# Eleven instead of eight attention chunks get q and k rearranged in DRAM and turned in 32x32 blocks on VectorE

## The chip, the cores and the metric

The kernel runs on one core of one Trainium2 chip. The metric is device time in microseconds for one execution of the whole program, as the median of several runs. The times of before are 1193.07 to 1195.81 us over nine runs, median 1193.97 us.

## What is computed

A block-wise linear attention with decay (batch 4, 8 heads, 768 tokens, head dimension 64) feeds a mixture of four two-layer experts over its 3072 output rows of 512 values. All data is fp32.

```python
# attention, per block of the sequence; the result is the same for any block length
intra = ((q_b @ k_b.T) * Dmask) @ v_b           # Dmask[i, j] = lam**(i-j) for i >= j
inter = (q_b * lam_pow) @ kv_state
out_b = intra + inter
kv_state = lam_block * kv_state + (k_b * rev_pow).T @ v_b
# bridge: (B, H, S, D) -> x of (B*S, H*D)
# experts: p = normalised domain_probs
for e in range(4):
    out += p[:, e:e+1] * (maximum(x @ w1[e], 0) @ w2[e])   # 512 -> 1024 -> 512
```

## The kernel before

**Tiling.** The 3072 tokens are 24 chunks `n` of 128 (`C`); a batch has 6 chunks (`NCH`), so chunk `n` is batch `b` and place `c` with `b, c = divmod(n, 6)`. Eight chunks make a group `g` (`CPG = 8`), three groups in all. A group's attention output, transposed, is the tile `xT` of 1024 columns, and the experts run on a group at a time as units `(g, e)`. Both expert products use Strassen's scheme with seven products (`M1` to `M7`); each first product is nested once more, so it reads seven 128x256 operand pieces of x and seven of w1. Those pieces are made once (on GpSimd or VectorE), stored to DRAM as `x_ops` and `w_ops`, and loaded again for each product.

**Order of the work.** The schedule is written out by hand. A loop goes over units, in each over seven products `i`, in each over eight slots `x`. A slot puts a few matmuls of the second product of this unit (L860) and of the first product of the next unit (L806) on TensorE, and then serves queues:

- `feed` (L733, L735) issues the loads `xs_in` and `ws_in` for the first product after next, once per product. Both tiles have two buffers, so a load waits until TensorE has read the tile of two products ago.
- `feed2` (L841) issues the two `w2t` loads of a later second product.
- `background`, through `rest()`, is one deferred piece of VectorE work per slot (the sums `hS` that the second product reads, masks, state updates). `soon` puts pieces at its head.
- `steps` is the attention of the next group: for each chunk `turn`, then `scores`, then `values`. `values` of chunk `n` is followed by `load_more(n + 2)`.
- `chores` and `pump` hand out GpSimd's preparation of weights and the stores of it.
- `results` issues the stores of finished output rows (L878).
- `trickle` issues one waiting `across` piece at every odd slot.

Nearly all DMAs are issued from SyncE (SP), in program order.

**The two ways of turning q and k.** The scores need q and k with the head dimension on partitions. In the ordinary way `load` (L123) brings q and k of a chunk with tokens on partitions; `turn` puts eight 128x128 transposes on TensorE (L530), into two PSUM banks, and ScalarE copies both to SBUF (L535, L536).

In the other way, taken by chunks with `comes_across(n)`, `bring_across(b)` lists 32 DRAM-to-DRAM copies for batch `b` (q then k; four quarters; four head pairs), which put 32x32 blocks of q and k where the later load wants them. Each copy (L367) covers all chunks from `ACROSS[b]` to the batch's end, in elements of 32 values (128 bytes). `load_across` (L384) brings `qx` and `kx` of a chunk, `turn_across` puts two `nc.vector.transpose` of 128x512 (L517) on VectorE, which turn the 32x32 blocks in place, and there is neither a TensorE transpose nor a ScalarE copy. Token-major `kn` and `vn` are loaded in both ways.

`bring_across(2)` is called before the last direct products of group 0, `bring_across(3)` at unit 3. If pieces still wait when a chunk of this kind is loaded, `load_more` issues all of them first:

```python
def load_more(n):
    if not comes_across(n):
        load(n)
    else:
        trickle(len(pieces))
        load_across(n)
        load(n, "kv")
```

DMAs issued from SP use eight semaphores in turn, so each waits for the landing of the eighth before it; a load of what another DMA has written to DRAM also waits for that landing.

Of the kernel before, what the change touches and what calls it, by code (L numbers as in the profile page):

```python
# [22 lines left out]
def kernel(  # L23
# [329 lines left out]

    ACROSS = {2: 2, 3: 2}
    across = dram.tile([B, 2, P, NHP, NCH * 4, 32], FP32, name="across")
    pieces = []

    def bring_across(b):  # L360
        c = ACROSS[b]
        for x, of in enumerate((q, k)):
            for y in range(4):
                for ac in range(NHP):
                    src = of[b, 4 * (y // 2) + ac, c * C:, (y % 2) * 32:(y % 2 + 1) * 32]
                    to = across[b, x, y * 32:(y + 1) * 32, ac, c * 4:]
                    pieces.append(lambda to=to, src=src: nc.sync.dma_start(  # L367
                        out=to, in_=src.rearrange("(t p) d -> p t d", p=32),
                    ))
# [6 lines left out]
    def comes_across(n):  # L376
        b, c = divmod(n, NCH)
        return b in ACROSS and c >= ACROSS[b]

# [986 lines left out]
```

## Time and profile before

| what | value |
|---|---|
| median of nine runs | 1193.97 us |
| the profiled execution's own time | 1193.68 us |
| its span | 1191.9 us |
| TensorE (PE) busy | 1179.3 us, 99% |
| weight loads (PEld) | 1023.3 us, 86% |
| VectorE (DVE) busy | 807.2 us, 68% |
| ScalarE (ACT) busy | 253.2 us, 21% |
| GpSimd (POOL) busy | 636.6 us, 53% |
| DMA queue of SP | 252144 packets, 320.40 MB, 81.1% of 16 engines |
| packets under 512 B | 117280 of 261783 |
| TensorE transposes of q and k (L530) | 128 in 16 chunks |
| VectorE block turns (L517) | 16 in 8 chunks |
| copies to `across` (L367) | 64 of 64 KB |

The span is what the profile covers, from the first instruction to the last; the run's own time lies 1.8 us above it. Matmuls are pipelined: the duration of one is longer than the distance from its start to the next one's start, and only the latter is time on TensorE.

### The profile page before, as it was taken

Reading aid. Unit: us, or ns where it says so; the run is one execution under the profiler, and the core shown is the slowest. Engines: PE = TensorE matmul, PEld = TensorE weight load, DVE = VectorE, ACT = ScalarE, POOL = GpSimd, SP = SyncE. Lnnn points to the kernel's source line nnn. Section 1 sums busy time; section 2 is a strip of 40 time slices with the busy share of each in tenths; the row PEclk is TensorE's granted clock in tenths of the full one; section 3 lists DMA queues with packets and bytes.
Section 4 is the critical chain, followed back from the end, with each engine's and each line's share of the span. In section 5 each row is a group of like instructions: output and inputs, shape, how many; then the busy total and the mean of one; then the engine's idle time right before and its main releaser. Section 6 shows DMA issues by size and latency. Waiting matters only on the chain.

```text
span 1191.9 us, 17827 instructions
## 1 busy us (share of the span) xinstructions
PE 1179.3 (99%) x6559; PEld 1023.3 (86%) x6559; DVE 807.2 (68%) x1334; ACT 253.2 (21%) x462; POOL 636.6 (53%) x600
## 2 busy tenths in 40 slices
PE   9998999999999999999999999999999999999998
PEld 8887888888888888888888888888888888888877
DVE  6597786477467857647756764764665676777784
ACT  3321121113201201311220120120143241240232
POOL 1966248449457900055244655415683683883884
PEclk9999999999999999999999999999999999999999
DMA  9896789999999997899997989998986657566542
GB/s 231 215 304 200 247 265 314 366 326 333 367 352 330 323 284 228 253 305 293 311 307 250 290 289 316 280 322 280 316 288 248 238 204 277 189 256 223 212 167 81
DMA packets 261783, 324.23 MB, mean 272 GB/s; under 512 B 117280, under 2 KB 203200, under 8 KB 261696
## 3 DMA queue, kind: packets, MB, share of 16 engines
q1 hardware_dynamic: 252144, 320.40, 81.1%
q10 hardware_dynamic: 9552, 2.69, 1.1%
q8 instruction: 52, 0.85, 0.3%
q14 instruction: 35, 0.29, 0.1%
HBM read 237.69 MB, written 89.54 MB: 275 GB/s over the span
## 4 chain that ended last, share of the span: by engine, by line
PE 86%; DVE 7%; DMA 2%; POOL 2%; issue 2%; ACT 0%; SPq 0%; ACTq 0%; DVEq 0%; POOLq 0%
PE pg L806 35%; PE q L860 29%; PE pq L1032 12%; DVE m L95 3%; PE sp L552 2%; DVE hS L95 2%; PE op L580 2%; PE pM L1124 1%; PE op L575 1%; POOL ops L95 1%; DVE xt L95 1%; PE op L588 1%; PE qp L530 1%; DMA w_ops<-w2o 1%; DMA w2b<-in_moe_w_dram 1%
## 5 line engine op out<-in xcount | busy, mean ns | idle before, releaser
L806 PE MATMUL pg<-xs_in,ws_in 128*128 128x256 f32 x1960 | 469.9, 380 | 1.7 <-DVE m L95 1.5
L806 PEld LDWEIGHTS pg<-xs_in,ws_in 128*128 128x128 f32 x1960 | 371.1, 190 | 54.4 <-DVE m L95 3.8
L95 DVE TENSOR_TENSOR m<-pg,m 128x512 f32<-128x512 f32 x451 | 307.9, 687 | 102.4 <-PE pg L806 94.4
L860 PE MATMUL q<-w2t,hS 128*128 128x256 f32 x1024 | 243.4, 380 | 0.0
L860 PEld LDWEIGHTS q<-w2t,hS 128*128 128x128 f32 x1024 | 193.2, 190 | 27.0 <-issue 0.2
L876 DVE SCALAR_TENSOR_TENSOR acc<-q,gate,acc 128x256 f32<-128x256 f32 x192 | 92.5, 482 | 169.6 <-PE q L860 169.3
L860 PE MATMUL q<-w2t,m 128*128 128x256 f32 x768 | 182.8, 381 | 0.0
L860 PEld LDWEIGHTS q<-w2t,m 128*128 128x128 f32 x768 | 144.7, 190 | 20.8 <-DVE m L95 0.4
L818 ACT ACTIVATE m<-m 128x512 f32<-128x512 f32 x132 | 83.0, 630 | 337.4 <-DVE m L95 332.8
L95 POOL TENSOR_TENSOR m<-m,xT 128x512 f32<-128x512 f32 x64 | 81.6, 1292 | 73.6 <-ACT m L818 55.2
L95 DVE TENSOR_TENSOR sums<-pq,sums 128x256 f32<-128x256 f32 x154 | 64.5, 422 | 45.7 <-PE pq L1032 39.9
L814 ACT COPY m<-pg 128x512 f32<-128x512 f32 x88 | 51.5, 586 | 177.7 <-PE pg L806 172.7
L95 POOL TENSOR_TENSOR kn<-kn,s_decay 128x512 f32<-128x512 f32 x20 | 23.8, 1191 | 120.1 <-DMA across<-in_k_dram 80.4
L1032 PE MATMUL pq<-acc,w2t 128*128 128x256 f32 x352 | 86.7, 379 | 0.5 <-POOL m L95 0.5
L95 DVE TENSOR_TENSOR m<-m,m 128x512 f32<-128x512 f32 x96 | 83.7, 875 | 0.0
L95 POOL TENSOR_TENSOR ops<-w2b 128x256 f32<-128x256 f32 x24 | 17.8, 762 | 117.3 <-DMA w2b<-in_moe_w_dram 116.4
L1032 PEld LDWEIGHTS pq<-acc,w2t 128*128 128x128 f32 x352 | 66.8, 190 | 9.9 <-POOL m L95 0.9
L753 ACT ACTIVATE m<-m 128x512 f32<-128x512 f32 x48 | 30.3, 631 | 167.6 <-DVE m L95 167.4
L95 DVE TENSOR_TENSOR hS<-m,m 128x512 f32<-128x512 f32 x64 | 54.6, 858 | 4.9 <-ACT m L818 4.9
L95 POOL TENSOR_TENSOR acc<-hT,hT 128x512 f32<-128x512 f32 x32 | 40.3, 1272 | 29.7 <-PE pq L1032 29.0
L95 POOL TENSOR_TENSOR w2o<-w2b 128x512 f32<-128x512 f32 x32 | 41.6, 1322 | 25.7 <-DMA w2b<-in_moe_w_dram 10.6
L95 POOL TENSOR_TENSOR acc<-hT,acc 128x512 f32<-128x512 f32 x32 | 40.7, 1273 | 7.4 <-PE pq L1032 5.4
(136 smaller groups left out, 1311.9 us busy)
## 6 DMA issues: line engine op xcount, KB each, us to landing
xs_in<-x_ops SPq DMA_DIRECT2D x70, 896.0 KB, 6.3
ws_in<-w_ops SPq DMA_DIRECT2D x70, 896.0 KB, 8.7
w2t<-w_ops SPq DMA_DIRECT2D x66, 256.0 KB, 6.7
w2t<-w_sums SPq DMA_DIRECT2D x64, 256.0 KB, 4.1
w_ops<-ops SPq DMA_DIRECT2D x28, 512.0 KB, 6.0
w2t<-in_moe_w_dram SPq DMA_DIRECT2D x48, 256.0 KB, 3.6
x_ops<-ops SPq DMA_DIRECT2D x17, 512.0 KB, 8.4
w2b<-in_moe_w_dram SPq DMA_DIRECT2D x32, 256.0 KB, 6.0
```

The costliest lines, as they stand in the source:

```text
L95: eng.tensor_tensor(out=o, in0=a, in1=b, op=op)
L530: nc.tensor.transpose(out=x[:, ac * C:(ac + 1) * C], in_=y[:, 2 * ac:2 * ac + 2].rearrange("p r d -> p (r d)"), identity=ident[:],)
L552: nc.tensor.matmul(out=sp[r][:, ac * C:(ac + 1) * C], lhsT=hc(kT)[half[r], ac], rhs=hc(qT)[half[r], ac], start=True, stop=True,)
L575: nc.tensor.matmul(out=op[r][half[x], a * C:(a + 1) * C], lhsT=kv[half[r], 2 * a + x], rhs=hc(qs)[half[r], 2 * a + x], start=(a == 0), sto ...
L580: nc.tensor.matmul(out=op[r][half[x], a * C:(a + 1) * C], lhsT=vn[:, 4 * r + 2 * a + x], rhs=hc(st[r])[:, 2 * a + x], start=(first and a = ...
L753: nc.scalar.activation(out=o[:], in_=o[:], func=AF.Relu)
L806: nc.tensor.matmul(out=p[:, j * 256:(j + 1) * 256], lhsT=ws[i][:, j * P:(j + 1) * P], rhs=xs[i], start=(fresh and j == 0), stop=True, skip ...
L814: nc.scalar.copy(out=new[at][:], in_=p[:])
L818: nc.scalar.activation(out=new[at][:], in_=new[at][:], func=AF.Relu)
L860: nc.tensor.matmul(out=p[:, s * DH:(s + 1) * DH], lhsT=h[A_OF[m]][:, c * 256 + s * P:c * 256 + (s + 1) * P], rhs=fed2[g, e, m][uu][:, c], ...
L876: nc.vector.scalar_tensor_tensor(out=o, in0=x, scalar=w, in1=o, op0=ALU.mult, op1=ALU.add)
L1032: nc.tensor.matmul(out=p[:, 0:256], lhsT=fed3[e, m, x // 2][:, x % 2, c * P:(c + 1) * P], rhs=b[B_OF[i]][:, c * 256:(c + 1) * 256], start= ...
```

## The change

One line is changed. It sets from which chunk of its batch on q and k come across.

```diff
-    ACROSS = {2: 2, 3: 2}
+    ACROSS = {2: 0, 3: 1}
```

Before, chunks 14 to 17 (batch 2) and 20 to 23 (batch 3) come across; after, also 12, 13 and 19. There are 64 copies to `across` as before, but each of the 32 for batch 2 covers six chunks instead of four (768 elements instead of 512), and each for batch 3 covers five instead of four (640 instead of 512). Since chunk 19 is loaded one chunk earlier than chunk 20, the copies of batch 3 that wait at that moment are issued there, one after the other.

## The prediction

> **What bounds the kernel now.** I read the page's busy times first, then the busy times by stretch, then TensorE's groups by shape, and last the timelines of PE and SP around the three chunks. For the whole span and for the stretches in which the three chunks are turned:
>
> ```profile
> PE 1179.3 (99%) x6559; PEld 1023.3 (86%) x6559; DVE 807.2 (68%) x1334; ACT 253.2 (21%) x462; POOL 636.6 (53%) x600
> ```
>
> ```profile
> 200.00:300.00 100.00, 100.00 (x629) 86.41 (x628) 63.50 (x103) 19.36 (x36) 62.67 (x66) 1.00 0.99 334
> 300.00:400.00 100.00, 99.87 (x610) 86.16 (x609) 68.29 (x108) 16.64 (x30) 63.09 (x61) 1.00 0.99 348
> 400.00:500.00 100.00, 99.50 (x547) 86.11 (x546) 65.92 (x109) 17.72 (x31) 15.72 (x17) 1.00 0.85 264
> 500.00:600.00 100.00, 100.00 (x609) 86.44 (x608) 64.77 (x107) 17.54 (x32) 42.04 (x47) 1.00 0.96 303
> ```
>
> The columns are the stretch, then us (and instructions) of PE, PEld, DVE, ACT and POOL, the granted clock and the DMA share. PE is full and at full clock, so what leaves PE shortens the run and what makes PE wait lengthens it. DMA at 0.99 is the second thing to watch. DVE at 0.64 to 0.68 has room. PE's idle time in the stretch from 300 to 700 us is small: its waits there are two, 1.0 us in all, both for a DVE evacuation.
>
> **Term 1: TensorE loses 24 transposes.** Groups by shape, and PE's timeline at a chunk that is still turned on PE:
>
> ```profile
> L530 PE MATMUL qp<-ident,qn 128*128 128x128 f32 x64 | 10.2, 283 | 0.0
> L530 PE MATMUL kp<-ident,kn 128*128 128x128 f32 x64 | 9.7, 274 | 0.0
> ```
>
> ```profile
> 492.81 1.89 PE L806 MATMUL pg<-xs_in,ws_in 128*128 128x256 f32 x8
> 494.54 0.60 PE L530 MATMUL qp<-ident,qn 128*128 128x128 f32 x4
> 494.98 0.60 PE L530 MATMUL kp<-ident,kn 128*128 128x128 f32 x4
> 495.41 1.89 PE L860 MATMUL q<-w2t,hS 128*128 128x256 f32 x8
> ```
>
> One transpose lasts some 280 ns, but they overlap: from the first (494.54) to the matmul after the eighth (495.41) it is 0.87 us, 109 ns each. The eight products ahead take 1.73 us (492.81 to 494.54), as always, so nothing else is hidden there. Three chunks free 3 x 0.87 = 2.6 us. The scores (L552) are the same instructions in both ways, so nothing is added to PE. I take this term at its full value, because PE is full at 272, 307 and 524 us, where chunks 12, 13 and 19 are turned.
>
> The Trainium skill (TensorE: Matmul & The Clock Gate, Part 4: PE-mode transpose) gives about 275 ns for a 128x128 transpose in a kernel's context. The duration in the rows agrees with it, but the distance from start to start does not; by the page, as an estimate, 24 x 275 ns would be 6.6 us. The sum goes by the 109 ns.
>
> ScalarE loses six copies of 0.59 us (L535, L536), and GpSimd's decay of `kn` no longer waits for PE. ScalarE is 21% busy, so both are worth nothing.
>
> **Term 2: VectorE gets six block turns.**
>
> ```profile
> L517 DVE STREAM_TRANSPOSE qx<-qx x8: 700/701/702, 339.4 to 653.7; 128x512 f32<-128x512 f32 x8
> L517 DVE STREAM_TRANSPOSE kx<-kx x8: 669/690/701, 340.6 to 655.0; 128x512 f32<-128x512 f32 x8
> ```
>
> Six at 0.70 us are 4.2 us, 1.4 us a chunk, put at the head of the deferred DVE work, so the sums `hS`, which the second product reads, come two slots later. After 307 us DVE idles 0.17 to 2.97 us ahead of each evacuation, 10 us in 14, and after 524 us nearly as much: there the cover is complete. After 272 us (chunk 12) it is 84 to 87% busy and the cover is thin. What it costs where the cover fails is in the trace: eight chunks already go this way, and while they do PE waits 1.0 us for DVE. If all of that is theirs, a chunk costs 0.12 us and three cost 0.4 us. Bounds: 0 (the cover holds), and 3 x 1.4 = 4.2 us (nothing hides); the second needs a full DVE, which the stretches exclude, so I use 0 to 1 us and take 0.4.
>
> **Term 3: more small packets on the DMA engines.** The copies to `across` get 32 x 256 + 32 x 128 = 12,288 more elements of 128 bytes. The trace has 32,768 such packets, 12.9 ns each on one engine, so the addition is 12,288 x 12.9 / 16 = 9.9 us of all 16 engines. Loading `qx` and `kx` (512 packets of 512 B each at 27.7 ns, 0.89 us) instead of q (1024 of 256 B at 18 ns, 1.15 us) adds 0.6 us a chunk. Two thirds of the 9.9 us fall between 63 and 176 us (share 0.80 to 0.86), where PE's few waits are for DVE, whose inputs are long there. SP is busy without a break from 63 to 83 us; ten longer copies push a store that GpSimd waits for (landing at 79.5 us) by some 2 us, and GpSimd's operands for the next products are ready 15 us early. I put that at nothing. In the full stretch from 200 to 400 us only the two bigger loads are new. The weight piece `ws_in` is the later half of each pair; across that stretch it lands 3.2 to 8.5 us before its first matmul, 3.2 us at the pair behind chunk 12's load. 0.6 us fits. Zero again, with 0 to 1.7 us as the range (chunks 12 and 13 give nothing if DMA were the limit).
>
> The Trainium skill (DMA: Bandwidth & Descriptors, Rules for kernel authors) says to coalesce small transfers, since below 64 KB one pays mostly overhead; that speaks against this change. Here the copies grow from 64 to 96 and 80 KB, so their per-copy part is paid no more often; it is the packet count that grows.
>
> **Term 4: the burst ahead of chunk 19.** This is the part that decides. SP's timeline where chunk 19 is loaded:
>
> ```profile
> 479.14 1.22 SPq L123 DMA_DIRECT2D qn<-in_q_dram  x2
> 480.40 1.73 SPq L123 DMA_DIRECT2D kn<-in_k_dram  x2
> 482.17 0.51 SPq L118 DMA_DIRECT2D vn<-in_v_dram  x1
> ...
> 485.09 1.08 SPq L841 DMA_DIRECT2D w2t<-in_moe_w_dram  x2
> 486.26 0.42 SPq L733 DMA_DIRECT2D xs_in<-x_ops  x1
> 486.73 0.42 SPq L735 DMA_DIRECT2D ws_in<-w_ops  x1
> ```
>
> In the changed program's instruction order ten copies of 640 elements come at 479.14, then `qx`, then `kx`, which waits for the landing of the ten, then `kn`, `vn`, an output store, two `w2t`, and only then `xs_in` and `ws_in` of the product that starts at 499.8 us. Before, that `ws_in` lands at 496.4 us, 3.4 us early. The queue drains in order: its last store lands at 482.3. Ten copies at 640 x 12.9 / 16 = 0.52 us are done at 487.5. `kx` is issued then; a DMA on an empty queue lands 2.3 us after its issue (the copy at 469.6), so the queue, with 0.9 us of `qx` left, runs dry for about 1 us and `kx` lands near 490.3. `kn` 1.15, `vn` 1.15, the store 0.4 and `w2t` 1.6 end at 494.6. From there to the landing of `ws_in` the pairs of before take 4.3 to 7.6 us, most near 5.3: 499.9, or 498.9 to 502.2. So PE waits 0.1 us, 0 to 2.4 us. Copies in a row may also issue more slowly than they drain: four took 3.45 us at 65.6 us and 5.64 us at 445.9. I add 0.7 us for that and take 0.8 us; the upper end is the rival below. A later pair has over 3 us left and meets no copies any more, so the loss comes once.
>
> **Sum.** -2.6 + 0.4 + 0 + 0.8 = -1.4 us. Against the profiled execution: 1193.68 - 1.4 = 1192.3 us; the median is 0.3 us above that execution, so 1192.6 us.
>
> **Rivals.** (a) The slack takes the burst and DVE hides its turns: only term 1 remains, 1193.97 - 2.6 = 1191.4 us. For it: ten copies cost 5.2 us of engine time against 3.4 us of slack, and q's load (1.15 us) is gone from the same place. Against it: `kx` must wait for all of them. (b) Slower: SP issues the ten copies no faster than three in a row at 507.9 to 511.9, 1.16 to 1.58 us each, mean 1.31. Then they end at 479.1 + 13.1 = 492.2 rather than 487.5 and PE waits 4.8 us: -2.6 + 0.4 + 4.8 = +2.6, 1196.6 us; with five quarters of that for 640 elements, 8 us of wait and 1199.8 us. It decides from about 1 us a copy on. Against it: those three stood behind three 512 KB loads, and the burst stands behind small stores. (c) DMA is the limit from 200 to 400 us: chunks 12 and 13 free 1.7 us of PE that then waits for operands, 1194.3 us. For it is the share of 0.99; against it, most pairs there are issued as soon as PE frees the buffer, so the queue catches up. (d) That it does not do what it says is excluded by the instruction order: 24 transposes fewer on PE, six on DVE more.
>
> **How the numbers follow.** A measurement of this kernel can tell about 0.2%, 2.4 us, from no change: faster is below 1191.6, slower above 1196.4. The forecast with its own range, 1191.7 to 1193.8, has 0.37; (a) 0.26; (b) 0.22; (c) 0.15. So faster 0.26, same 0.52, slower 0.22. The range goes from (a) less the 0.4 us by which runs scatter, 1191.0, into (b), 1197.5.
>
> **What would show it.** Right: L530 x104 in all instead of 128, at 109 ns apart; L517 x22; a PE wait at about 499 us of about 1 us whose operands are `xs_in`, `ws_in`, with SP's `ws_in` issued near 491; nothing new at 272 and 307 us. Wrong in term 4: ten L367 issues from 477 us on that end before 485 us, or after 491. Wrong in term 2: PE waits for DVE between 265 and 290 us. Wrong in term 3: pairs between 200 and 400 us that land after PE could use them.

## The result, and the profile after

The changed kernel takes 1200.03 us (median of 9 runs, 1197.96 to 1202.37); the kernel before, run beside it on the same chip, 1194.16 us (29 runs). The ratio is 1.0046, 95% interval 1.0038 to 1.0055: slower by 5.9 us, where the prediction had 1192.6 us and a range up to 1197.5. The profiled execution takes 1198.8 us with a span of 1197.0 us, against 1191.9 us before: 5.1 us of the difference can be read in the two traces.

Of the changed kernel: the page's busy times, groups by shape (busy us, mean ns of one, idle time before them), and the busy times by stretch (stretch, then us and instructions of PE, PEld, DVE, ACT and POOL, the granted clock, the DMA share, GB/s):

```profile
PE 1180.4 (99%) x6535; PEld 1022.7 (85%) x6535; DVE 810.8 (68%) x1340; ACT 250.0 (21%) x456; POOL 635.0 (53%) x600
```

```profile
L530 PE MATMUL qp<-ident,qn 128*128 128x128 f32 x52 | 8.4, 287 | 0.0
L530 PE MATMUL kp<-ident,kn 128*128 128x128 f32 x52 | 8.1, 279 | 0.0
L517 DVE STREAM_TRANSPOSE qx<-qx 128x512 f32<-128x512 f32 x11 | 7.7, 701 | 0.0
L517 DVE STREAM_TRANSPOSE kx<-kx 128x512 f32<-128x512 f32 x11 | 7.6, 688 | 0.0
```

```profile
200.00:300.00 100.00, 100.00 (x626) 86.35 (x625) 63.82 (x104) 18.54 (x35) 62.49 (x66) 1.00 0.99 342
300.00:400.00 100.00, 99.76 (x604) 85.68 (x602) 71.36 (x112) 15.45 (x28) 65.06 (x64) 1.00 1.01 351
400.00:500.00 100.00, 98.58 (x541) 85.38 (x541) 65.98 (x110) 17.98 (x32) 14.78 (x16) 1.00 0.87 261
500.00:600.00 100.00, 97.01 (x566) 83.56 (x567) 62.08 (x102) 14.51 (x27) 41.22 (x47) 0.97 0.89 288
...
500.00:510.00 10.00, 7.01 (x20) 5.71 (x21) 1.46 (x4) 1.17 (x2) 0.00 (x0) 0.66 1.02 392
```

PE has 24 instructions fewer, DVE six more, as the edit says, and yet PE is busy 1.1 us longer. The groups by shape show the same: 24 transposes fewer, six block turns more, each at its old duration. From 200 to 400 us nothing is wrong: PE is busy 0.11 us less than before there. The damage lies in 400 to 600 us, and the last row narrows it down: in the ten microseconds from 500 PE is busy 7.01, and its granted clock is 0.66. Before, the same hundred microseconds from 500 had 100.00 and 1.00. PE's timeline there (start, duration, what it waited for in brackets):

```profile
496.98 1.89 PE L860 MATMUL q<-w2t,m 128*128 128x256 f32 x8
498.70 0.27 PE L466 MATMUL gp<-ident,gate 128*32 128x128 f32 x1
502.99 3.75 PE L806 MATMUL pg<-xs_in,ws_in 128*128 128x256 f32 x8 [4.01 <-DMA ws_in<-w_ops]
506.54 2.90 PE L860 MATMUL q<-w2t,m 128*128 128x256 f32 x8
509.27 1.89 PE L806 MATMUL pg<-xs_in,ws_in 128*128 128x256 f32 x8
```

In the kernel before, the same product starts without a wait:

```profile
499.73 0.27 PE L466 MATMUL gp<-ident,gate 128*32 128x128 f32 x1
499.84 1.89 PE L806 MATMUL pg<-xs_in,ws_in 128*128 128x256 f32 x8
```

There are two losses in a row. PE waits 4.01 us for `ws_in`. Then eight products that always take 1.89 us take 3.75, and the next eight 2.90: the matmuls start 427 ns apart instead of 216 until the clock is back. SP's timeline shows why `ws_in` was late:

```profile
477.73 0.33 SPq L878 DMA_DIRECT2D out_dram<-acc  x1
478.11 7.99 SPq L367 DMA_DIRECT2D across<-in_k_dram  x10
486.14 0.64 SPq L384 DMA_DIRECT2D qx<-across  x1
488.95 0.56 SPq L384 DMA_DIRECT2D kx<-across  x1
489.56 1.16 SPq L123 DMA_DIRECT2D kn<-in_k_dram  x2
490.77 0.51 SPq L118 DMA_DIRECT2D vn<-in_v_dram  x1
491.32 0.94 SPq L878 DMA_DIRECT2D out_dram<-acc  x1
492.31 1.03 SPq L841 DMA_DIRECT2D w2t<-in_moe_w_dram  x2
493.44 0.41 SPq L733 DMA_DIRECT2D xs_in<-x_ops  x1
493.89 0.43 SPq L735 DMA_DIRECT2D ws_in<-w_ops  x1
```

The ten copies keep SP for 8 us, 0.80 each, and the last lands at 488.90 us; `kx`, which reads what they wrote, is issued at 488.95. `ws_in` is issued at 493.89 instead of 486.73 and lands at 502.85 instead of 496.4.

Where the 5.1 us come from is read by setting each product's start beside the same product's start before:

| Part of the trace | PE later than before by | at its end |
|---|---|---|
| up to 179 us (start, copies of the first batch) | +0.72 us | +0.72 |
| chunk 12 turned on DVE, 273 us | -0.87 | -0.15 |
| chunk 13, 308 us | -0.88 | -1.03 |
| 308 to 500 us: the wait of 4.01 us and 0.17 us of small shifts | +4.18 | +3.15 |
| half clock, 13 matmuls at 427 ns | +2.83 | +5.98 |
| chunk 19, 525 us | -0.88 | +5.10 |

After that the difference stays where it is to the end.

### The profile page after: what moved, and what is told of

Read it like the earlier page. It is cut to its first block, busy times and chain, and to the rows that moved or that the text cites. A ratio compares the mean times of both kernels' runs of the same rounds, so it can differ in the third digit from the quotient of the medians.

```text
span 1197.0 us, 17775 instructions
## 1 busy us (share of the span) xinstructions
PE 1180.4 (99%) x6535; PEld 1022.7 (85%) x6535; DVE 810.8 (68%) x1340; ACT 250.0 (21%) x456; POOL 635.0 (53%) x600
## 4 chain that ended last, share of the span: by engine, by line
PE 84%; DVE 5%; SPq 4%; DMA 3%; POOL 2%; issue 1%; ACT 0%; ACTq 0%; DVEq 0%; POOLq 0%
PE pg L806 36%; PE q L860 31%; PE pq L1032 12%; DVE m L95 2%; PE sp L552 1%; DVE hS L95 1%; PE op L580 1%; SPq L123 1%; POOL w2o L95 1%; DMA w2b<-in_moe_w_dram 1%; SPq L341 1%; DMA ws_in<-w_ops 1%; PE op L575 1%; SPq L367 1%; DMA across<-in_q_dram 1%
## 5 line engine op out<-in xcount | busy, mean ns | idle before, releaser
L95 POOL TENSOR_TENSOR ops<-w1b 128x256 f32<-128x256 f32 x24 | 20.3, 867 | 47.6 <-PE pg L806 24.0
```

What stands on the lines that cost most here:

```text
L95: eng.tensor_tensor(out=o, in0=a, in1=b, op=op)
```

## The experiments

All ratios are to the kernel before, run beside each kernel on the same chip. "Ahead" and "behind" at a place mean the start of the same product in the trace of before; at 179 us it is the matmul that starts there at 178.88 us.

### Which chunk costs it: 12 and 13 alone, 19 alone

```diff
-    ACROSS = {2: 2, 3: 2}
+    ACROSS = {2: 0, 3: 2}      # chunks 12 and 13 alone
+    ACROSS = {2: 2, 3: 1}      # chunk 19 alone
```

> Chunks 12 and 13 come across, chunk 19 does not (ACROSS {2: 0, 3: 2}). Theory A (the loss is the burst of copies ahead of chunk 19 and TensorE's half clock after the wait that it makes): no burst, so the two chunks give their 2 x 0.87 us: 1.7 us faster than before, at least 1.0 us if the 0.6 us that TensorE was late at 179 us in the changed kernel belongs to the bigger copies. Rival B (the larger copies and the VectorE turns cost all along): no gain, or slower by 0.5 to 2 us, with new TensorE waits between 60 and 310 us. Rival C (clock falls for another reason): says nothing here.

> Only chunk 19 is added (ACROSS {2: 2, 3: 1}). Theory A: the whole loss is here: a wait of about 4.1 us near 500 us, then about 13 matmuls at 427 ns instead of 216 ns (2.8 us), less 0.87 us: 6.0 us slower than before. Rival B: the loss is spread, so less than half of it is here: 0 to 3 us slower.

Chunks 12 and 13 alone: 1193.61 us, ratio 0.9995 (0.9986 to 1.0003). In its trace PE is 0.53 us behind at 179 us and 1.22 us ahead after chunk 13. Chunk 19 alone: 1199.75 us, ratio 1.0048 (1.0036 to 1.0061), with a wait of 3.47 us at 499.6 us and half clock for some eight matmuls. The whole loss belongs to chunk 19. The first two chunks free what the prediction said, but part of it is lost again before 179 us.

### The burst without the hold, and the hold put behind the pair

The first kernel is before, with the ten copies that wait at the place of chunk 19's load (of 512 elements here) issued there, although chunk 19 does not use them; there is no `kx` to wait for them. The second is the changed kernel, with `qx` and `kx` of chunk 19 issued behind the next `xs_in` and `ws_in`.

```diff
 def load_more(n):
+    if n == 19:
+        trickle(len(pieces))          # burst alone, on before
```

```diff
         trickle(len(pieces))
-        load_across(n)
+        if n == 19: put_off.append(lambda: load_across(n))   # run after the next feed
+        else: load_across(n)
         load(n, "kv")
```

> Before's eight chunks; only the waiting copies (of 512 elements) are all issued ahead of chunk 19's load, which stays the ordinary one, so no load waits for their landing. If the burst's issue time on SP (0.64 us or more for each of ten) is the delay, ws_in is issued 3 to 5 us later than before and TensorE waits 0.5 to 2 us near 500 us: 0.5 to 4 us slower (the upper end with a half clock). If the wait of kx for the copies' landing is what matters, the queue never runs dry, ws_in lands within 3.4 us of before and nothing is lost: within 0.5 us of before.

> The changed kernel with the burst, but chunk 19's qx and kx are loaded after the next xs_in and ws_in instead of ahead of them, so that SP does not stand in kx's wait with the operand loads behind it. If the wait is the larger part: ws_in issues 3 to 4 us earlier than in the changed kernel, TensorE waits less than 1 us, no half clock: 1 to 2.6 us faster than before. If the burst's length is enough: still a wait of 2 us or more near 500 us, and slower than before.

The burst alone: 1195.31 us, ratio 1.0015 (1.0002 to 1.0028). Its `ws_in` is issued at 491.38 us, 4.65 us later than in before, and PE waits 1.52 us. In the changed kernel the issue is 7.16 us late, so the copies are some 4.6 us of it and `kx`'s hold, with the queue standing idle behind it, some 2.5 us. SP issues these copies of 512 elements 0.67 us apart, practically as far as those of 640 (0.68 us), though their packets are only 0.41 us of the engines (512 x 12.9 ns / 16): the time of a burst is SP's for each copy, not that of its bytes. With `kx` put behind: 1193.85 us, ratio 0.9997 (0.9987 to 1.0006), with one wait of 2.02 us at 500 us and no half clock:

```profile
502.19 1.97 PE L811 MATMUL pg<-xs_in,ws_in 128*128 128x256 f32 x8 [2.02 <-DVE hS L95]
503.99 1.89 PE L865 MATMUL q<-w2t,m 128*128 128x256 f32 x8
```

The row names a sum on VectorE, but it is again `ws_in` that ends the wait: it lands at 502.05 us, 0.14 us ahead of the product, as in the changed kernel (502.85 and 502.99). Here the products behind the wait take 1.97 and 1.89 us. PE waits 2.0 us less, and the 2.8 us of half clock are gone as well. Against before the run is 6.2 us better than the changed kernel; these two explain 4.8, and the spans of the two profiled executions differ by 3.2 only, because this one was 0.5 us further behind at 179 us and had waits of 0.3 and 0.5 us for `ws_in` at two other pairs (256 and 342 us).

### Is the half clock made by the wait?

The changed kernel, with matmuls that nobody reads in the place of the wait:

```diff
+    if at == 4 and i == 0 and x == 1:
+        idle = bank("s1", "fp")
+        for _ in range(17):           # 34 in the first version
+            nc.tensor.matmul(out=idle[:, 0:P], lhsT=ident[:], rhs=ident[:], start=True, stop=True)
```

> The changed kernel with 34 dummy 128x128 matmuls (109 ns each, 3.7 us; their result is read by nobody) put on TensorE just where it waits near 499 us. Theory A, with the half clock being the consequence of TensorE's idle time: the wait for ws_in is as long, but TensorE is busy in it, no matmul at 427 ns follows, and the run is 2.8 us faster than the changed kernel, about 2 to 3 us slower than before. Rival C (the clock falls without regard to TensorE's idle time, by load or by time): the 427 ns stay and the time is that of the changed kernel, 5 to 6 us slower than before.

> The changed kernel with 17 idle 128x128 matmuls on TensorE ahead of the first product of the unit in which it waited 4.0 us (two records of 112 ns each, so 17 x 0.224 = 3.8 us: about what the wait was; their results are read by nobody). Theory: the 2.8 us of half clock come from the wait itself, because TensorE had nothing to do for over 3 us; with the gap filled, the matmuls after it are 216 ns apart at once, the start of the product stays at about 503.0 us, and the run is some 2.8 us shorter than the changed kernel's 1200.0: 1197.2 us, ratio 1.0027 to before. Rival: the clock falls for another reason (the DMA load or the state of the chip at that moment), 427 ns stay, and the run takes 1200 us.

The first version: 1200.09 us, ratio 1.0050 (1.0038 to 1.0062). Each dummy made two matmul records, so they filled 7.6 us instead of 3.8, and PE started the product 3 us after `ws_in` had landed; half clock there was none. The second, with half as many, 1196.43 us, ratio 1.0026 (1.0016 to 1.0037): 2.8 us behind before where the changed kernel is 5.9 behind. PE's timeline of it, and the stretches:

```profile
503.16 3.96 PE L1312 MATMUL fp<-ident 128*128 128x128 f32 x34
507.35 1.97 PE L806 MATMUL pg<-xs_in,ws_in 128*128 128x256 f32 x8 [0.23 <-DMA ws_in<-w_ops]
509.15 1.89 PE L860 MATMUL q<-w2t,m 128*128 128x256 f32 x8
```

```profile
500.00:510.00 10.00, 9.78 (x62) 8.84 (x62) 3.55 (x6) 2.49 (x5) 0.09 (x1) 1.00 1.03 375
```

`ws_in` is no earlier for it (it still ends the last 0.23 us of the wait), but the clock stays at 1.00 where it was 0.66, and the products take 1.97 us at once. So the half clock is made by PE standing idle, and it cost 2.8 us of the changed kernel's time. The rest of the wait is still there.

### The copies begun earlier

The batch's copies begin in the last product of the unit before, and go two for one in two places of the next.

```diff
-        if at == 3: bring_across(3)
+            if at == 2 and i == 6: bring_across(3)
-                    trickle()
+                    trickle(2 if at == 3 and i in (2, 4) else 1)
```

> The changed kernel, but the copies of batch 3 begin in the last product of unit 2 and two are issued at a time in two products of unit 3, so that none is left when chunk 19 is loaded. The same copies, the same eleven chunks. Theory A: no wait near 500 us, full clock; all three chunks give their 0.87 us: 1.9 to 2.6 us faster than before. Rival B: the number of packets and the VectorE turns are unchanged, so it stays slower than before or equal to it.

1194.49 us, ratio 1.0011 (1.0002 to 1.0021). No wait is left at 500 us, but there is a new one, of the same kind, at the pair behind the eight copies that now come from 434 to 449 us (four in the changed kernel): `ws_in` is issued at 451.23 instead of 446, PE waits 2.89 us, and eight products take 2.98 us instead of 1.89. The burst was not removed, it was moved to a pair with less slack (2.8 us in before, against 3.4 at 500 us).

### VectorE's cover

Chunks 12 and 13 alone, with their block turns done three times over:

```diff
-        soon(n, *(lambda x=x: nc.vector.transpose(out=x[:], in_=x[:]) for x in (qT, kT)), scaled)
+        soon(n, *(lambda x=x: turned_block(x) for x in (qT, kT)), scaled)   # three times for n in (12, 13)
```

> As with chunks 12 and 13 alone, but their block turns are done three times over (the same result), so 8 more VectorE instructions of 0.70 us, 5.6 us. If VectorE hides its turns (my term 2 at 0 to 0.4 us): the time of the run with chunks 12 and 13 alone within 0.5 us. If the turns lie on the path: 2 to 5 us more than that run, with TensorE waits for VectorE near 275 and 310 us.

1196.65 us, ratio 1.0020 (1.0011 to 1.0030). The scores of chunk 12 now wait, those of chunk 13 do not:

```profile
281.51 1.16 PE L556 MATMUL sp<-qx,kx 64*128 64x128 f32 x16 [2.25 <-issue]
```

At chunk 12 the cover holds 1.4 us of turns and not 4.2; at chunk 13 it holds 4.2. In the changed kernel neither waits, and the scores of chunk 12 start at 277.8 us, right behind the products ahead of them. The prediction was right that the thin place was chunk 12.

### The bigger copies alone

Before, with the copies of the first batch covering all six chunks, though chunks 12 and 13 are still turned on TensorE:

```diff
-        c = ACROSS[b]
+        c = {2: 0, 3: 2}[b]
```

> Before's eight chunks; the 32 copies of batch 2 cover six chunks instead of four (and those of batch 3 five... no: four, as before), and nobody reads the added part. It has the added packets of batch 2 alone (8192 of 128 B), with no transposes saved. If the packets are free (my term 3): the time of before within 0.5 us. If they cost: 0.5 to 2 us slower, and TensorE late by 0.6 us at 179 us as in the changed kernel.

1195.11 us, ratio 1.0006 (0.9996 to 1.0015): by the runs no difference that can be told from none. The trace shows where the time goes: PE is 1.17 us behind at 179 us. The first of GpSimd's sums in that stretch, which wait for a store (`w_sums`) that SP issues among the copies, starts at these times: in the kernel before, in the changed kernel, in this one, and in a later one (below) that issues no copies from 63 to 78 us:

```profile
79.62 2.96 POOL L95 TENSOR_TENSOR w2o<-w2b 128x512 f32<-128x512 f32 x2 [10.46 <-DMA w_sums<-w2o]
```

```profile
81.09 2.96 POOL L95 TENSOR_TENSOR w2o<-w2b 128x512 f32<-128x512 f32 x2 [13.63 <-DMA across<-in_q_dram]
```

```profile
82.08 2.95 POOL L95 TENSOR_TENSOR w2o<-w2b 128x512 f32<-128x512 f32 x2 [13.96 <-DMA w_sums<-w2o]
```

```profile
74.64 2.50 POOL L95 TENSOR_TENSOR w2o<-w2b 128x512 f32<-128x512 f32 x2 [7.65 <-DMA w_sums<-w2o]
```

In the second row a copy is named, but there too the store lands just ahead, at 80.97 us. By 179 us PE in these four is at 0, +0.72, +1.17 and -2.71 us: about half a microsecond for each by which GpSimd starts earlier or later. Identical code also differs here from run to run. Over nine traces with the changed kernel's copies at the start, this one among them, PE is at -0.4 to +2.1 us, 1.0 us in the mean, and at +4.16 in a tenth where a wait at 106 us brought half clock; over three with the copies of before it is at -0.4 to 0. So a single figure is worth little, and the cost is some 1.2 us in the mean rather than the 0.7 of the changed kernel's trace.

### Two copies for one where SP waits

The changed kernel, with six of the ten copies put into the places between output stores ahead of the burst (four are left for it); then the same with the hold put behind the pair, as above.

```diff
-                    trickle()
+                    trickle(2 if at == 3 and i in (4, 5) else 1)
```

> The changed kernel, with two copies instead of one in each place of the last stretch before chunk 19's load (six copies more between 456 and 475 us, where SP waits between output stores; four instead of ten are left for the burst). Theory: the burst lasts some 3 us instead of 8, the copy that kx waits for lands by 484, ws_in is issued at 488 to 489 and lands at about 497.5, two us ahead of its use: no wait of TensorE, no half clock; 2.5 us freed less 0.7 at the start give 1192.1 us, ratio 0.9985. Rival: the six copies take from the slack of the pair ahead (5.4 us at 485) what the burst took before, TensorE waits there, and the run takes 1194 us or more, as with the copies begun in the earlier unit (1194.5).

> The changed kernel with both cures of the burst: two copies for one between 456 and 475 us (four copies left for the burst), and chunk 19's qx and kx loaded behind the next pair xs_in, ws_in, so that the pair no longer stands behind kx's wait for the copies. Theory: what is left of TensorE's wait with two for one alone (1.5 us) is the gap in the queue that kx's wait makes (issue of kx to landing of ws_in was 13.9 us both times); without it ws_in is issued at about 488.5 and lands at 497.5, TensorE does not wait at 499.8, and the run takes 1192.3 us, ratio 0.9985. Rival: the engines simply have more to carry in this stretch, ws_in lands past 500 us again, and the run takes 1194 us.

Two for one: 1194.15 us, ratio 1.0004 (0.9996 to 1.0013); with the hold away as well 1193.43 us, ratio 0.9998 (0.9989 to 1.0007). The first still waits 1.53 us at 500 us: its last copy is issued by 484.4 and `kx` at 486.67, and from there to the landing of `ws_in` it is 14.0 us, against 13.9 in the changed kernel. In the second `ws_in` lands at 499.67, no more than 1 us earlier, since the copies two at a time are held up too (2.7 us for two at 479 us). PE does not wait there at all, but in this trace it also came 2.1 us later to the place, so this pair of runs alone does not show that the hold was the rest. The last version below speaks for it: there PE comes 5 us earlier than in before and does not wait either. It comes out level with before and not 1.4 us faster as expected, since PE in its trace was 1.1 us behind at 179 us (GpSimd's sums started at 82.02 us) and lost another 0.7 us at 238 us. So the burst was cured, and the other loss was left.

### The copies of the start moved

Three versions move the first batch's copies out of SP's stretch from 63 to 78 us: the first lets them come later, one at a time, to about 205 us (chunks 12 and 13 alone); the second is the changed kernel with this and two for one; the third (chunks 12 and 13 alone) issues two for one in the next unit instead, so that all are out by about 155 us.

```diff
-            if m in SEQ0[-2:]:
-                trickle()
...
-                    trickle()
+                    trickle(2 if at == 0 else 1)     # the third version only
```

> Before plus chunks 12 and 13 on VectorE, and the copies of that batch issued only from the next unit on (the ten that SP issued between 63 and 78 us go to the end of the row, some 173 to 205 us; chunk 12 is loaded at 226 us). Theory: the 0.7 us (0.3 to 1.5) that kernels with the bigger copies lose by 179 us come from SP's full stretch from 63 to 83 us, which delays a store that GpSimd waits for. Without copies there GpSimd starts its sums at 75 to 76 us rather than at 79.6 (before) or 81 (changed), the waits at 100 to 105 us shrink, and the run takes 1192.3 us (two transposed chunks, 1.64 us, less nothing): ratio 0.9986. Rival: the cost is the transfers themselves on the DMA engines; they are only moved to the stretch where their share is 0.99, and the run takes 1193.6 us as the plain kernel with chunks 12 and 13 did, or more.

> All eleven chunks, with both moves: no copy between 63 and 78 us, and two for one between 456 and 475 us. Theory: the three chunks' 2.5 us come whole, and the start's loss is gone: 1191.4 us, ratio 0.9978. Rival: late copies of the first batch collide in the full stretch around 200 us: then as the kernel with two for one alone, 1192 us, or 1193.5 us.

> Before plus chunks 12 and 13 on VectorE; the ten copies between 63 and 78 us are gone, and the next unit issues two copies for one, so that all 32 are issued between some 80 and 155 us and none between 173 and 205 us. Theory: the loss at the start (0.7 us by 179 us) comes from SP's full stretch from 63 to 83 us, and the waits at 253 us of the version whose copies came late (1.1 to 5.1 us) from the copies past 173 us; here neither is left: GpSimd starts at 75 to 77 us, TensorE is ahead of before by 1 to 2 us at 179 us and by 3 us past 307 us; the run takes 1191.5 us, ratio 0.998. Rival: two for one delays the stores of the operands (x_ops, w_ops) between 110 and 155 us and TensorE's later loads with them: 1193.6 us or more.

The first: 1193.42 us, ratio 1.0000 (0.9990 to 1.0011), its runs 1190.22 to 1197.48. The second: 1197.62 us, ratio 1.0027 (1.0010 to 1.0044), 1191.85 to 1203.01. The third: 1190.67 us, ratio 0.9973 (0.9962 to 0.9983), 1189.12 to 1191.58. In the first PE is 2.24 us ahead at 179 us, as the theory said, and then loses more than that at one pair:

```profile
249.95 1.89 PE L860 MATMUL q<-w2t,m 128*128 128x256 f32 x8
256.93 3.53 PE L806 MATMUL pg<-xs_in,ws_in 128*128 128x256 f32 x8 [5.09 <-DMA ws_in<-w_ops]
```

The copies now fall just ahead of the stretch whose DMA share is 0.99, and this pair, which had 0.3 us of slack in the changed kernel, lands late. The second version's profiled execution waits 1.10 us at the same pair. Why its other runs scatter so far was not seen in a trace; a wait that sometimes passes into half clock is argued, not shown. The third has no wait there: both the theory of the start and the rival of the first trial were right, each in its place.

### All of it, and what the change itself is worth

All eleven chunks, with the start's copies two for one in the next unit, two for one between 456 and 475 us, and chunk 19's `qx` and `kx` behind the pair; and, on one chip with its repetition, the eight chunks of before with the start's move alone.

> All eleven chunks with the three moves together: the first batch's copies between 80 and 155 us, the second's two for one between 456 and 475 us, and chunk 19's qx and kx behind the pair. Theory: three chunks' 2.5 us come whole and the start gains 1 to 2 us: 1190.5 us, ratio 0.997. Rival: one of the moves costs what it frees: 1192.5 to 1194 us.

> Before with its eight chunks, only the first batch's copies moved: none between 63 and 78 us, two for one in the next unit. Theory: the move alone is worth the 2.8 us that the version with ten chunks was ahead of before at 179 us, and the chunks' own saving comes on top: 1191.2 us, ratio 0.998; beside it the version with all eleven chunks and the three moves has 1189.2 us (1.5 to 2.5 us less). Rival: the move frees the same 1.6 us that the chunks free (the start is bound by something else), and eight chunks take 1193 us.

> The version with all eleven chunks and the three moves again, on the same chip as the one with eight chunks and the first move. Theory: 1189.5 us, ratio 0.9966 to before, and 1.5 to 2.5 us less than eight chunks with the move. Rival: the three chunks bring nothing once the start is mended: both the same.

| Kernel | median us | ratio to before |
|---|---|---|
| eleven chunks, all moves | 1189.56 | 0.9966 (0.9954 to 0.9978) |
| eight chunks, start moved | 1191.81 | 0.9983 (0.9974 to 0.9992) |
| eleven chunks, all moves, again | 1188.72 | 0.9958 (0.9945 to 0.9970) |

This version beats both kernels: 4.8 us less than before on the last chip, and by medians 11 us less than the changed kernel (each against before beside it). SP's and PE's timelines of the last run at the place of the burst:

```profile
478.09 2.60 SPq L367 DMA_DIRECT2D across<-in_k_dram  x4
480.74 1.18 SPq L123 DMA_DIRECT2D kn<-in_k_dram  x2
...
484.70 0.42 SPq L740 DMA_DIRECT2D ws_in<-w_ops  x1
485.18 0.58 SPq L384 DMA_DIRECT2D qx<-across  x1
485.80 1.62 SPq L384 DMA_DIRECT2D kx<-across  x1
```

```profile
494.77 0.27 PE L471 MATMUL gp<-ident,gate 128*32 128x128 f32 x1
494.88 1.89 PE L811 MATMUL pg<-xs_in,ws_in 128*128 128x256 f32 x8
```

`kx` waits 1.62 us with nothing urgent behind it, and PE goes from the gate's transpose to the next product in 0.11 us, where the changed kernel needed 4.3. In this run PE is 2.32 us ahead of before at 179 us, and then gains 0.87, 0.88 and 0.88 us at chunks 12, 13 and 19: 2.6 us, the prediction's term 1. The two kernels of the same chip differ by 3.1 us, of which these 2.6 are the change's own worth; the move of the start, which has nothing to do with the number of chunks, gives the eight chunks 1.75 us (2.26 us ahead at 179 us in its trace).

## Why the prediction was wrong

**Term 1, 24 transposes: right.** 0.87, 0.88 and 0.88 us for the three chunks in the changed kernel, 2.6 us as the sum had it, at the places named, because PE was full there. The distance from start to start was the right price and the single transpose's duration the wrong one.

**Term 2, block turns: right**, 0.4 us predicted and nothing seen. The cover at chunk 12 is as thin as it looked: three times the turns made a wait of 2.25 us there.

**Term 3, small packets: wrong by 0.7 us at the start, right later in the profiled run but not by much.** From 200 to 400 us the changed kernel's trace shows no price, as predicted. That was close: the pair behind chunk 12's load landed 0.3 us ahead of its first matmul, where it had 3.2 us in before and 0.6 us more of load was counted. In four of the eight traces whose program is the same up to there, PE waits 0.2 to 1.2 us for `ws_in` at one or two of the pairs of 256 and 342 us. So "Zero again, with 0 to 1.7 us as the range" was right in its range, and the zero was in part luck. At the start the failed step is "GpSimd's operands for the next products are ready 15 us early. I put that at nothing." SP's push of the store was seen and sized (2 us; GpSimd starts 1.5 us later in the changed kernel's trace and 2.5 with the bigger copies alone), but followed only to the next products and not to the chain of GpSimd, VectorE and PE behind it, which at 92 to 106 us has PE waits of 0.4 to 1.7 us in before already. That this chain carries the delay on is read from the four rows above and from the kernels that moved the copies away, where both GpSimd and PE came earlier. A place where PE already waits has no slack, whatever one operand's margin is.

**Term 4, the burst: the right place, the right chain, the wrong size: 4.0 us of wait for 0.8.** The failed step is "Ten copies at 640 x 12.9 / 16 = 0.52 us are done at 487.5": it took the engines' time where SP's was the longer. Where nothing holds them the copies are issued 0.68 us apart, in the burst 0.80 in the mean (two stood for 1.2 and 1.4 us), and the last lands at 488.90, 2.8 us after SP is through with it. From the first copy to `kx`'s issue it took 10.8 us (478.11 to 488.95) where the prediction had 8.4 (479.1 to 487.5). The order of the later steps held: `kx` goes out at once when the copies land, and `kn`, `vn` and `w2t` follow. But from there to the landing of `ws_in` it took 13.9 us where the sum had 12.4 (487.5 to 499.9). These 2.5 and 1.5 us make the 4.0 us of wait where the chain gave 0.1; the 0.7 us added for slow issue were too few. `ws_in` was issued 2.9 us later than the "near 491" of the prediction and landed at 502.85 for 499.9, although PE, and the burst with it, came 1.0 us earlier than in before. Rival (b) had the sign and, with "PE waits 4.8 us", nearly the size. Its condition, "from about 1 us a copy on", was wrong: 0.8 us a copy was enough, since the last copy's landing and the steps behind `kx` took longer as well. That its larger figure, 1199.8 us, is nearly the time measured is chance: it has 8 us of wait and no half clock. The bound that was to show term 4 wrong (copies that end "before 485 us, or after 491") was too wide for a pair with no slack left: they ended at 486.1.

**What was not in the sum at all: the half clock.** The prediction priced a PE wait at its own length. This one cost 4.0 + 2.8 us. Without it, with the same wait, the changed kernel would have taken 1197.2 us by this estimate, just inside the range; the filled kernel took 1196.4. The Trainium skill (TensorE: Matmul & The Clock Gate, Why this matters for your kernels) tells not to leave PE idle for more than some 3 us between bursts, since an idle window returns it to half clock, and gives the window as 3413 ns, free-running (Part 1). The runs agree on the window: half clock lasted 3.4 us or twice that, and its 427 ns are twice the 216. On the limit the runs are less kind than the page: 1.8 us of idleness within one window was enough, as worked out below. Of the 7.4 us by which the median was missed, the traces hold 6.5: 3.2 are term 4, 2.8 the half clock, 0.7 term 3, 0.2 small shifts, less term 2's 0.4. The other 0.9 us lie in the scatter between the profiled executions and the medians.

## What to carry to other kernels

A wait that is added ahead of a full TensorE is to be priced twice: by its length, and, from about 2 us on, by the half clock that may follow it: in these runs that hung on where the wait lay in a fixed grid of 3.41 us, which a prediction does not know, so it is a chance and not a term. Count a burst of small DMAs by the time the issuing queue needs for each, and put whatever must wait for them behind the loads that TensorE needs next, not ahead of them. When a step is moved or made longer, look along the path for the place where the bounding engine already waits: the slack of one operand elsewhere does not cover that place.

## What was not expected of the hardware

- **When idleness halves the clock.** The length of a wait does not decide it alone. Waits of 1.5 to 1.7 us (in eleven traces) and of 1.91, 2.02, 2.25 and 2.48 us left the clock at full. Waits of 1.92 us (in one trace of the eleven chunks with all moves), 2.08, 2.89, 3.47 and 5.09 us brought 3.4 us of half clock, the one of 4.01 us 6.8 us. What separates them in the traces is a fixed grid. In the changed kernel's trace the granted clock becomes full at 6.81 us, half at 501.75 and full at 508.57: 494.94 and 6.82 us, which are 145 and 2 times 3.413 us. With the late copies it changes at 4.10, 256.68 and 260.10 us, 74 and once 3.413 us apart. With each trace cut into such windows from its first change on, all 19 agree: where PE stood idle for 1.80 us or more of a window at full clock (six times), the next window ran at half; where it stood idle for 1.67 us or less, it did not. The wait of 1.92 us had 1.80 in one window; those of 1.91, 2.02, 2.25 and 2.48 us fell into two, with 1.56, 1.02, 1.31 and 1.64 us in the larger part. Half clock went on for a second window where 1.24 us of the first was idle, and ended where 0.25 us was. Such windows (us and instructions of PE, PEld, DVE, ACT and POOL, granted clock, DMA share, GB/s) of the changed kernel, of the wait of 1.92 us and of that of 1.91 us:

```profile
498.33:501.75 3.42, 0.65 (x4) 0.23 (x2) 2.38 (x4) 0.45 (x2) 0.00 (x0) 1.00 0.95 307
501.75:505.16 3.41, 2.17 (x5) 1.83 (x6) 0.00 (x0) 0.09 (x1) 0.00 (x0) 0.50 1.07 410
505.16:508.57 3.41, 3.41 (x9) 2.65 (x9) 0.00 (x0) 1.08 (x2) 0.00 (x0) 0.50 1.01 416
```

```profile
91.23:94.64 3.41, 1.61 (x6) 1.16 (x7) 3.41 (x6) 1.16 (x2) 0.77 (x1) 1.00 0.45 175
94.64:98.06 3.42, 3.42 (x9) 2.67 (x9) 3.38 (x7) 1.70 (x4) 0.00 (x0) 0.50 1.07 284
```

```profile
92.46:95.87 3.41, 1.84 (x7) 1.35 (x8) 3.41 (x6) 1.26 (x2) 3.25 (x4) 1.00 1.02 338
95.87:99.28 3.41, 2.98 (x14) 2.33 (x13) 3.38 (x5) 2.12 (x4) 3.41 (x3) 1.00 0.90 245
```

- **A burst of copies of 640 elements of 128 bytes** cost SP 0.68 us each where nothing held them, more than the 0.52 us that the engines' packets add up to, and 2.7 us for two where more was waiting to land (477.8 us in the two-for-one kernel).
- **A 128x128 fp32 matmul against the identity** as an ordinary product left two records, 34 for 17, with 3.96 us for all; the same shape as a transpose leaves one, 109 ns from the next.
